# Another order table for a kernel of masked attention and a gated MLP

## The chip, the cores and the metric

The kernel runs on one core of a Trainium2 chip. The metric is the device time of one execution in microseconds (us). The kernel before takes 935.06 us, the median of three runs (934.54 to 935.51).

## The reference

The kernel computes masked attention, with two kinds of masks, and then a normalised, gated MLP over all 4608 tokens, all in f32:

```python
B, H, S, D = 8, 8, 576, 64                 # batch, heads, positions, head size
scores = q @ k.T / sqrt(D)
mask_local   = (rel >= 0) & (rel < 32)     # heads 0 to 3; rel = row - column
mask_strided = (rel >= 0) & (col % 32 == row % 32)   # heads 4 to 7
attn = softmax(where(mask, scores, -1e9))
x = (attn @ v), heads side by side         # 4608 tokens x 512
rms = sqrt(mean(x * x, axis=-1) + 1e-6)
xn = x / rms * rms_g
g = xn @ w_gate                            # 512 x 1536
silu = g / (1 + exp(-g))
out = (silu * (xn @ w_val)) @ w_out        # 1536 x 512
```

## The kernel before

**The work.** A core has five engines with a queue each: PE (matrix products), DVE and POOL (element by element), ACT (functions of one operand, copies) and SP (which here issues transfers). The attention is done in 32 iterations of one batch and two heads each. An iteration has the scores on PE (`scores`, L289), a softmax (`soft`: mask L309, maximum L312, exponentials on ACT L316, reciprocals of the sums L320 and L321, product L323, transpose L325) and the product with the values on PE (`values`, L301). What comes out is copied into three ring buffers `raw`, as chunks of 512 tokens. Nine chunks then go through the MLP. For each, the squares are added over the four column slices (`ssq`, L422), the row statistics are formed on PE (L431), followed by a root and four reciprocals (L484), and each slice is scaled (L488) and split into a high and a low part (xh and xl; for chunk 0 L508 and L515), since each f32 product is done as three products of parts.

**The MLP.** The first chunks use plain products. For each of twelve units of 128 columns there is a gate product and a value product (`gemm1`, L541), the gate's scaling for chunk 0 (L551), tanh on ACT (L554), the gate (L556), the product with the values (L592) and its split (L599 or L601, and L608), and then the output product (L617). For chunk 0, one more PE product spreads the row statistics over all rows (L472), and ACT copies it out (L475) for L551. While chunk 0 runs, the weights are still decoded: for each weight tile some bit operations on DVE (L1747 and L1752), the high part on ACT (L1757) and the low part by a subtraction (L1759), after which SP stores the tile to DRAM (L1763, the output weights wos at L1766). Later chunks go in pairs, which need seven products instead of eight, with sums and differences of weights made on the way: `transform_gv` (L668, L672) and `transform_o` (loads L800 and L806, sums L808), split at L756 and L762 and stored to DRAM (tg, L770). In these pairs the products stand at L1594, copies and sums of results at L1612 to L1649, and copies of weights at L1303, L1309 and L1368. The chunks at the end have similar lines from L901 to L1170.

**The order.** Every operation is put into a list, with the tiles it reads and writes, and with one or several engines that can do it (`op` in `Plan`; `also` names the others). For each step the table `ORDER` names which of the operations that are left comes next, and on which engine, and the kernel's instructions are issued in that order: each engine works through its own instructions in it. So the table sets three things, the place of each instruction in its engine's queue, the engine of those operations that have a choice (most of DVE's and POOL's element operations and many copies of ACT), and the order of the transfers on SP. It was encoded as text and is read in `order`:

```python
code = zlib.decompress(base64.b85decode(ORDER))
left, out = list(range(n)), []
for k in range(n):
    i = left.pop(code[k] + 256 * code[n + k])
    out.append(self.ops[i][0][ENGINES[code[2 * n + k]]][2])
```

Of the kernel before, what the change touches and what calls it, by code (L numbers as in the profile page):

```python
# [25 lines left out]
P = 128  # L26
# [37 lines left out]
    "Dh7t2KA{&wcm3oB8uM^0x=ye87J5bS|`CyD|X$AC;f9Px!C;_N%wgymbFdFP=s($K{uf<Q{r9eDImj+E^=CPx%{99fXg62L$W>V~;N1eB}D%wcOH^k3C^M9$HtXgB#Yh"
    "r5oScTDrRX#;J4Pau%*^E;yGi4mjtpHqTAD-j&UXP48mi!dT&)+xT|==84?!mUn%{+vtvUgTc$*@Md)6e6+GYG`AT&JaFm4z=cjcefG@s>8R1E)E}rkI6QD-{lp=Ec<5"
    "*?t{*Pf4j(@BFKe|!>;77}u^8@OsMMF2Dof49%4#*7Z^d)frMMB-N6O*u>IaRxv)#sY<Ne8A<Gu0mcgI&6W6Q1m<&}D~zEr5!_7rL#6=$l?m*eNke=$*c=9&0P{LbaK<"
    "M7h+w{ZC5QmN6%7f)@~tU`SI)OTa&nacP5@^{PeccKa{8pWuPFWrc?2BSg{MnMz?`JkLH6{GyATEOl%!qUkTN5bIPnPB;6!M-Ti$S<A<gZsm3GdL0i>-nKlaIn~k+J)9"
# [1833 lines left out]
```

## Time and profile before

| | |
|---|---|
| median of three runs | 935.06 us (934.54 to 935.51) |
| the profiled execution, its own time | 938.68 us |
| its span | 936.9 us |
| instructions | 21775 |
| mean granted clock of PE | 0.983 of full speed |

The profile is of one execution. Times in it are counted from the start of its span. An engine's busy time is the time in which it had an instruction under way. A timeline's row is an instruction, or a run of equal ones (x2): its start, its time, its engine, line, operation and tiles, and in brackets how long the engine had been idle before and what ended that. Where this text speaks of the 2.4 and the 1.2 GHz of PE, these are granted clocks of 1.0 and 0.5.

### The profile page before, as it was taken

To read this page: it belongs to the slowest core of one execution; us is meant where nothing else is said; L and a number is where in the kernel's file an instruction comes from. 1 tells how busy PE (TensorE), PEld (TensorE's weight loads), DVE (VectorE), ACT (ScalarE), POOL (GpSimd) and SP (SyncE) were. 2 spreads that over 40 slices of the span, in tenths; PEclk is the share of its full clock that TensorE was granted. 3 is DMA by queue.
4 is the path that set the end of the run, shared out by engine and by line. 5 is a ranking of instruction groups with operands and counts; after the bars stand their busy time and mean duration, and the time that the engine had idled before them with its cause. 6 is when DMAs were issued, how large, how long until landed. Compare 5 with 4: busy or idle time off the path is not lost.

```text
span 936.9 us, 21775 instructions
## 1 busy us (share of the span) xinstructions
PE 907.5 (97%) x8708; PEld 733.7 (78%) x8708; DVE 758.8 (81%) x1224; ACT 464.9 (50%) x1312; POOL 263.0 (28%) x220
## 2 busy tenths in 40 slices
PE   4999998999999999999999999999999999999998
PEld 3877876877788787888887878888888888888786
DVE  5999998879978999897668999536569994458893
ACT  6898774434335468354344675433445642232210
POOL 1322231224413344445016224200170241112320
PEclk7699999999999999999999999999999999999999
DMA  8797338695766888936884579765564796575643
GB/s 287 273 366 265 114 119 310 241 347 199 257 249 200 287 288 262 377 132 216 278 295 137 175 249 328 273 245 175 191 223 153 233 344 222 183 267 194 202 157 112
DMA packets 95092, 220.76 MB, mean 236 GB/s; under 512 B 9616, under 2 KB 28688, under 8 KB 94992
## 3 DMA queue, kind: packets, MB, share of 16 engines
q1 hardware_dynamic: 94560, 218.83, 67.4%
q8 instruction: 68, 1.11, 0.5%
q10 hardware_dynamic: 432, 0.56, 0.2%
q14 instruction: 32, 0.26, 0.1%
HBM read 172.17 MB, written 47.19 MB: 234 GB/s over the span
## 4 chain that ended last, share of the span: by engine, by line
PE 66%; DVE 10%; DMA 2%; issue 1%; ACT 1%; POOL 1%; SPq 0%; DVEq 0%; ACTq 0%; POOLq 0%
PE acc L1594 10%; PE acc L1393 7%; PE v L1594 6%; PE g L1594 6%; PE g L1393 5%; PE v L1393 5%; PE g L1005 3%; PE v L1005 3%; PE acc L1005 3%; PE acc L541 3%; PE v L541 2%; PE v L1170 2%; PE g L1170 2%; PE pair L289 2%; PE acc L1170 2%; PE g L541 2%
## 5 line engine op out<-in xcount | busy, mean ns | idle before, releaser
L541 PE MATMUL g<-xh,wg 128*128 128x512 f32 x184 | 60.9, 413 | 6.8 <-DVE e L556 6.8
L316 ACT ACTIVATE pT<-pT,mx 128x64 f32<-128x64 f32 x160 | 53.6, 339 | 23.1 <-DVE mx L312 23.1
L541 PE MATMUL v<-xh,wv 128*128 128x512 f32 x184 | 57.9, 396 | 0.3 <-DVE e L592 0.3
L316 ACT ACTIVATE pp<-pp,mx 128x64 f32<-128x64 f32 x160 | 53.6, 340 | 8.8 <-DVE mx L312 8.7
L541 PEld LDWEIGHTS g<-xh,wg 128*128 128x128 f32 x184 | 35.4, 198 | 16.3 <-DVE e L556 8.8
L289 PEld LDWEIGHTS pair<-xx,xx 64*32 64x32 f32 (+1 forms) x2432 | 28.0, 109 | 19.4 <-issue 12.0
L289 PE MATMUL pair<-xx,xx 64*32 64x64 f32 (+1 forms) x2432 | 34.2, 234 | 7.0 <-issue 3.1
L541 PEld LDWEIGHTS v<-xh,wv 128*128 128x128 f32 x184 | 33.8, 188 | 8.0 <-DVE e L592 0.9
L541 PE MATMUL g<-xl,wg 128*128 128x512 f32 x92 | 37.1, 403 | 0.0
L541 PE MATMUL v<-xl,wv 128*128 128x512 f32 x92 | 35.9, 390 | 0.0
L672 POOL TENSOR_TENSOR tt<-tt 128x256 f32<-128x256 f32 (+1 forms) x25 | 20.8, 840 | 48.6 <-DVE tt L672 28.4
L541 PE MATMUL acc<-xh,wg 128*128 128x512 f32 x104 | 33.7, 406 | 0.8 <-DVE hl L556 0.8
L541 PE MATMUL acc<-xh,wv 128*128 128x512 f32 x104 | 33.4, 402 | 0.0
L359 ACT COPY raw<-pair 128x128 f32<-128x128 f32 (+8 forms) x60 | 19.3, 370 | 26.5 <-PE pair L301 26.4
L617 PE MATMUL acc<-or,hh 128*128 128x512 f32 x96 | 30.2, 396 | 0.8 <-DVE e L556 0.8
L316 ACT ACTIVATION_READ_ACCUMULATOR pp<-pp,mx 128x1 f32 x160 | 30.7, 192 | 0.0
L316 ACT ACTIVATION_READ_ACCUMULATOR pT<-pT,mx 128x1 f32 x160 | 30.6, 191 | 0.0
L1594 PE MATMUL acc<-wg,wv 128*128 128x512 f32 x102 | 29.1, 394 | 0.0
L1594 PE MATMUL acc<-wv,wv 128*128 128x512 f32 x102 | 28.7, 389 | 0.0
L1612 ACT ACTIVATE or<-g 128x512 f32<-128x512 f32 x24 | 14.4, 599 | 21.9 <-PE g L1594 18.2
L301 PEld LDWEIGHTS pair<-pp,vt 32*64 32x64 f32 x784 | 18.1, 139 | 8.8 <-issue 6.2
L554 ACT ACTIVATE e<-g 128x512 f32<-128x512 f32 x23 | 13.8, 599 | 22.3 <-PE g L541 17.4
(860 smaller groups left out, 2936.1 us busy)
## 6 DMA issues: line engine op xcount, KB each, us to landing
wv<-wsv SPq DMA_DIRECT2D x36, 512.0 KB, 6.9
wg<-wsg SPq DMA_DIRECT2D x26, 512.0 KB, 7.5
or<-tg SPq DMA_DIRECT2D x22, 512.0 KB, 5.8
th<-tg SPq DMA_DIRECT2D x21, 512.0 KB, 6.5
tl<-tg SPq DMA_DIRECT2D x21, 512.0 KB, 6.2
xx<-in_qT_dram SPq DMA_DIRECT2D x32, 288.0 KB, 5.3
xx<-in_kT_dram SPq DMA_DIRECT2D x31, 288.0 KB, 6.1
wg<-wos SPq DMA_DIRECT2D x32, 256.0 KB, 4.8
```

The costliest lines, as they stand in the source:

```text
L289: nc.tensor.matmul(out=pair_[32 * y:32 * y + m, h, 64 * g:64 * g + 64], lhsT=q[r, PAD + a:PAD + a + m], rhs=k[r, a:a + 64], start=True, st ...
L301: nc.tensor.matmul(out=dst[z // 2][64 * h:64 * h + 64, z % 2, 320 + c:320 + f], lhsT=v[r, 6 * h + j], rhs=t[r, a:a + f - c], start=j == fi ...
L316: nc.scalar.activation(out=tv[:, g], in_=tv[:, g], func=AF.Exp, bias=m[:, g:g + 1], accum_out=z[:, g:g + 1])
L359: nc.scalar.copy(out=d, in_=s)
L541: nc.tensor.matmul(out=out, lhsT=wt[:, w, sl], rhs=xhl[x, kc], start=(n == 0 and i == 0), stop=(n == KC - 1 and i == 2))
L617: nc.tensor.matmul(out=acc[t], lhsT=x[h][:, sl], rhs=wt[:, w], start=(u == 0 and i == 0), stop=(u == NU - 1 and i == 2))
L672: elementwise(width, lambda e: both(e).tensor_tensor(out=dst(), in0=a(), in1=b(), op=ALU.subtract), [], keys)
L1005: nc.tensor.matmul(out=banks[bk], lhsT=w, rhs=X[a, k].tile(y), start=start and k == 0 and i == 0, stop=stop and k == 1 and i == 2, skip_gr ...
L1170: nc.tensor.matmul(out=banks[bks[j]], lhsT=tile(v, k, j), rhs=x.tile(y), start=start and k == 0 and i == 0, stop=stop and k == KT - 1 and ...
L1393: nc.tensor.matmul(out=banks[bks[j]], lhsT=w.tile(v, k, j), rhs=x.tile(k, y), start=start and n == 0 and i == 0, stop=stop and n == KT - 1 ...
L1594: nc.tensor.matmul(out=banks[bk], lhsT=w, rhs=xtile(a, k, y), start=start and k == 0 and i == 0, stop=stop and k == 1 and i == 2, skip_gro ...
L1612: op("ACT", act(CH, True), 0, lambda: nc.scalar.activation(out=temp(dst), in_=banks[bk], func=AF.Copy, scale=scale), reads=bank_keys(bk), ...
```

## The change

The table `ORDER` is replaced. The new text is 56 lines long where the old had 57, so that every line behind it has a number lower by one. The 3612 operations, the tiles and the engines that each can use are the same; 358 operations are on another engine, and in each queue places change. The diff, cut to the first lines of the table, whose text tells a reader nothing by itself:

```diff
 ENGINES = ("PE", "DVE", "ACT", "Pool", "SP")
 ORDER = (
-    "c-rk)*>fDnd7nP#zILuXXD{q777OCO2m%B_kRU*c6iMjdO@fqY5)7?_vTQ37C0nu%$C50`vJ#a;>ONvwNja`c;#BN%Ra}+#yre2m`3q8c$wQvf(>=4G-t&?wG<GqVp6;"
...
+    "c-rk)S(jYZbw2wHcb><ZtGcSXyLukf>XB|qprIupK}$jiB!L9N!ZaX^g)Bp2GiZUq3^L1xfN?OyU<L<59OohN%F5y)$wMBqR(?nFmX(*Bd(OSpt^5JM^u5(x_ug~PK70"
...
```

PE's queue near the start, before: in the program's names xh0 and xl0 are the two parts of the first slice of chunk 0, xh2 and xl2 those of the next; wg0 and wv0 the first unit's weights; L301 the value products of an iteration.

```order
L289 MATMUL pair_72<-xx4_84,xx3_83 32x64 x36
L541 MATMUL acc2_70<-xh0_548,wv0_355 128x512 x2
L541 MATMUL acc2_70<-xl0_597,wv0_355 128x512
L541 MATMUL g_67<-xh0_548,wg0_532 128x512 x2
L541 MATMUL g_67<-xl0_597,wg0_532 128x512
L301 MATMUL pair_72<-pT0_97,vt0_85 64x32 x2
...
L541 MATMUL acc2_70<-xh2_618,wv0_355 128x512 x2
L541 MATMUL acc2_70<-xl2_665,wv0_355 128x512
L406 MATMUL v_68<-few_65,ssq_101 128x4 x4
L406 MATMUL v_68<-few_65,srt_102 128x4 x4
L541 MATMUL g_67<-xh2_618,wg0_532 128x512 x2
L541 MATMUL g_67<-xl2_665,wg0_532 128x512
```

The same two places now:

```order
L288 MATMUL pair_72<-xx4_84,xx3_83 32x64 x36
L540 MATMUL g_67<-xh0_535,wg0_529 128x512 x2
L540 MATMUL g_67<-xl0_542,wg0_529 128x512
L300 MATMUL pair_72<-pT0_97,vt0_85 64x32 x2
...
L540 MATMUL acc2_70<-xh0_535,wv0_549 128x512 x2
L540 MATMUL acc2_70<-xl0_542,wv0_549 128x512
L405 MATMUL v_68<-few_65,ssq_101 128x4 x4
L405 MATMUL v_68<-few_65,srt_102 128x4 x4
L540 MATMUL acc3_71<-xh1_759,wg1_560 128x512 x2
L540 MATMUL acc3_71<-xl1_773,wg1_560 128x512
```

The group on the first value weights (acc2 from xh0 and wv0) has moved from ahead of these value products to behind the next ones. On DVE the L1759 that finishes wv0 has moved from row 15 of the queue to row 47. Behind the two statistics products (L406) PE now goes on with another slice (xh1).

DVE's queue where PE's longest wait ends, before: tt, th0 and tl0 belong to the weight sums, ssq and srt to the statistics of chunk 1, g and e to the gate of chunk 0.

```order
L762 TENSOR_TENSOR tl0_1849<-tt_105,th0_1826 128x512
L422 TENSOR_TENSOR ssq_101<-ssq_101,srt_102 128x512
L309 SCALAR_TENSOR_TENSOR pp0_95<-pair_72,cb_63 128x640
L312 TENSOR_REDUCE mx0_73<-pp0_95 128x10
L808 TENSOR_TENSOR tt_105<-tt_105,or4_1818 128x512
L484 RECIPROCAL srt_1949<-srt_1949 128x128 x3
L551 TENSOR_TENSOR g_67<-g_67,tl1_99 128x512
L672 TENSOR_TENSOR tt_105<-tt_105 128x256 x2
L556 SCALAR_TENSOR_TENSOR e_100<-e_100,g_67 128x512
L592 SCALAR_TENSOR_TENSOR e_100<-e_100,v_68 128x512
```

The same piece now:

```order
L421 TENSOR_TENSOR ssq_101<-ssq_101,srt_102 128x512
L761 TENSOR_TENSOR tl0_1861<-tt_105,th0_1857 128x512
L308 SCALAR_TENSOR_TENSOR pp0_95<-pair_72,cb_63 128x640
L311 TENSOR_REDUCE mx0_73<-pp0_95 128x10
L483 RECIPROCAL srt_1954<-srt_1954 128x128 x3
L550 TENSOR_TENSOR g_67<-g_67,tl1_99 128x512
L483 RECIPROCAL srt_1954<-srt_1954 128x128
L555 SCALAR_TENSOR_TENSOR e_100<-e_100,g_67 128x512
L591 SCALAR_TENSOR_TENSOR e_100<-e_100,v_68 128x512
```

The sum of squares comes ahead of the split, the L808 and the two L672 have left this piece, and the fourth reciprocal stands between L550 and L555.

SP's queue at the loads of the output weights wos2 and wos3, which the weight sums need, before:

```order
L1763 DMA wsg0_119<-wg0_532 128x1024
L800 DMA tt_105<-wos2_109 128x2x256
L770 DMA tg7_150<-th0_1826 128x1024
L800 DMA tt_105<-wos3_110 128x2x256
L1763 DMA wsv5_130<-wv5_1075 128x1024
```

And now:

```order
L272 DMA vt0_85<-in_vl_dram 128x768
L799 DMA tt_105<-wos2_109 128x2x256
L799 DMA tt_105<-wos3_110 128x2x256
L769 DMA tg7_150<-th0_1857 128x1024
L262 DMA xx0_80<-in_kT_dram 128x576
```

The second load has moved ahead of the store of tg7.

## Rows read from the trace of the kernel before

**Rows 1.** The page: span, and each engine's busy us, share, instructions.

```profile
span 936.9 us, 21775 instructions
...
PE 907.5 (97%) x8708; PEld 733.7 (78%) x8708; DVE 758.8 (81%) x1224; ACT 464.9 (50%) x1312; POOL 263.0 (28%) x220
```

**Rows 2.** Stretches: us, busy PE, PEld, DVE, ACT, POOL, PE clock, DMA, GB/s.

```profile
0.00:50.00 50.00, 36.52 (x800) 29.00 (x801) 37.71 (x79) 38.27 (x126) 11.82 (x24) 0.73 0.80 289
50.00:150.00 100.00, 93.32 (x1064) 72.49 (x1062) 95.45 (x149) 80.06 (x207) 25.72 (x20) 1.00 0.62 216
150.00:200.00 50.00, 47.99 (x427) 38.80 (x428) 41.48 (x70) 20.72 (x76) 13.59 (x14) 0.97 0.82 293
200.00:650.00 450.00, 447.08 (x4874) 361.78 (x4873) 376.88 (x602) 225.50 (x690) 145.42 (x112) 1.00 0.71 245
650.00:700.00 50.00, 50.00 (x296) 41.13 (x296) 30.50 (x49) 21.06 (x54) 19.32 (x15) 1.00 0.62 205
```

**Rows 3.** Timeline from 147 to 152 us: DVE, then ACT, then PE.

```profile
147.76 0.70 DVE L551 TENSOR_TENSOR g<-g,tl 128x512 f32<-128x512 f32 x1 [0.45 <-PE g L541]
149.66 0.88 DVE L672 TENSOR_TENSOR tt<-tt 128x256 f32<-128x256 f32 x2 [1.20 <-POOL tt L808]
150.46 0.68 DVE L556 SCALAR_TENSOR_TENSOR e<-e,g 128x512 f32<-128x512 f32 x1
...
151.78 0.94 DVE L484 RECIPROCAL srt<-srt 128x128 f32<-128x128 f32 x1
...
148.49 0.60 ACT L554 ACTIVATE e<-g 128x512 f32<-128x512 f32 x1 [0.85 <-DVE g L551]
...
151.20 1.20 PE L541 MATMUL g<-xh,wg 128*128 128x512 f32 x2 [3.48 <-DVE e L556]
```

**Rows 4.** Stretches around changes of PE's clock, columns as in rows 2.

```profile
31.80:38.60 6.80, 6.58 (x195) 5.91 (x186) 6.47 (x12) 5.89 (x16) 1.04 (x1) 1.00 0.61 190
38.60:45.40 6.80, 6.80 (x21) 5.64 (x21) 6.21 (x20) 6.05 (x11) 3.00 (x2) 0.50 1.02 405
...
151.20:154.60 3.40, 3.40 (x8) 2.72 (x9) 3.37 (x6) 1.14 (x2) 0.94 (x2) 0.51 0.97 360
```

**Rows 5.** Timeline of PE, and a row of DVE, from 28 to 48 us.

```profile
28.65 1.22 PE L541 MATMUL acc<-xh,wv 128*128 128x512 f32 x2
...
39.88 1.20 PE L541 MATMUL g<-xh,wg 128*128 128x512 f32 x2
...
45.98 1.05 PE L472 MATMUL acc<-pT,few 128*128 128x128 f32 x8
...
47.69 0.70 DVE L551 TENSOR_TENSOR acc<-acc,tl 128x512 f32<-128x512 f32 x1 [1.69 <-ACT tl L475]
```

**Rows 6.** Timeline of DVE at 190 and of PE at 198 us.

```profile
189.75 0.69 DVE L808 TENSOR_TENSOR tt<-tt,or 128x512 f32<-128x512 f32 x1 [4.14 <-DMA tt<-wos]
...
197.78 0.73 PE L541 MATMUL g<-xh,wg 128*128 128x512 f32 x2 [0.81 <-DVE e L556]
```

**Rows 7.** Timeline of PE: four single waits after 200 us.

```profile
253.85 0.73 PE L541 MATMUL acc<-xh,wg 128*128 128x512 f32 x2 [0.75 <-DVE hl L556]
...
498.92 0.72 PE L1594 MATMUL g<-xh,or 128*128 128x512 f32 x2 [0.88 <-ACT or L1612]
...
511.40 0.50 PE L1594 MATMUL v<-xh,th 128*128 128x512 f32 x1 [0.79 <-DVE tt L1644]
...
870.06 0.96 PE L1170 MATMUL acc<-wg,wv 128*128 128x512 f32 x3 [0.53 <-DVE hl L1035]
```

**Rows 8.** DVE and POOL at 54 us; groups of DVE, 50 to 150: busy us, mean ns.

```profile
54.28 1.83 DVE L1752 SCALAR_TENSOR_TENSOR th<-or 128x512 uint32<-128x512 uint32 x1
...
54.27 1.30 POOL L1759 TENSOR_TENSOR wg<-tt,wg 128x512 fp32r<-128x512 f32 x1 [2.75 <-ACT wg L1757]
...
L1752 DVE SCALAR_TENSOR_TENSOR th<-or 128x512 uint32<-128x512 uint32 x11 | 8.7, 787 | 0.3
...
L1752 DVE SCALAR_TENSOR_TENSOR tt<-wg 128x512 uint32<-128x512 uint32 x8 | 5.4, 678 | 0.1
```

More of the change, by code (lines that the diff above doesn't have):

```diff
@@ L64 @@
[L64 to L67, printed above, removed]
@@ new lines @@
+    "7~xA!fCS*ZKEY7yO1bd50bASL|U(_HPIA84nZ(X7bQnBlocH;p5za#>N8^ZGg6dq~j~$7bZDYo0NvMvXgz^BYH1)%VnclXP;wGHyG^Za+ZxIgGCTw`I~`-@g9|13E}=Y"
+    "k2>4Ta&UqjFoSz?5d29xK%Qj{%6}6OwCToG2>=0b!^|PN0#5L{7W!Yx4!NEVIlr~?Qh#PYqqsN`N}H)uKrp4dF{(j|G4nUKg8AQ$A3@%@KN&ZugCs*sQgcZAN;Z0{W2-"
+    "FKdZj;Y4xj5CcbKYO~3f-FXAshAN@S8_kL?eI{kP!(CEOgK6v~7_dj0ytEBQ#bK=8aP58h3CGCFD{fqZU=H7hoW$)t8I}2|Q&)*E+NUnIVb-mSBZr=U!%<XS>e){^pj{"
+    "j=7`0~r?IC(cvUU+YWc~@?>pL{bt^Hy;9r%wEnXZ+~F8&5xY;?)=055=!+RPVY$&NSWUPnUnRSg($(|Dg43@0siF-OsH)?T$Tj`<18CeTSa#H#d(S-21%;FQ@*MCn`_)"
@@ new lines @@
+    "k9(!>dTW={dmr@{9t$3OX!YUBg^Rlv8xI8KbH{@F?z{N#+=YwL-026VS?}!8`x3GloSulD7(MyO$xC}5E??Sncq%v)otwDyov5{RCK(+}*3S33XE%C@eedkFcVej8Y#u"
+    "*8a92EVtWs~TA6{Q?R%+|(hvM3P@YTJ+{PB8etrWy7K|H;f?ru*0Zf>%fHl{vVYBthxTpvkhI<=vhca!RPw>tK-@lh7`SgE==xG-2PEhg!FnCuFlOQ(OB#_uN4=+*f9B"
+    "gyyPIGbEa?tAsV>#u}yT&ulse|)lfDSoJ;m!oT?(!X6TRn(}IcuBk&hv}n(!FQ4{jl+vk7=@K{l_(89n<|ILV?7AQ%YmQzNhdkvA3Sx)Kj7cJKlYCW{?Q<*4jl?g-QW&"
+    "C92w}X4Xk!LD=RCVc&Y6-hXQ|(@3&VxueDh5=1bmOEtpM$>FHo9IO<Kbz4ZleG>mp>b$8J9b<eh)UTjay&bs5%u083r?Xgp1?r3Wy=_T{SiCY_tJFRNn+k4P!ta-f)r4"
@@ new lines @@
+    "?^2wUf^BylwNvVcn@YRi|P{rJ>s30hf<B14$Y?jg}WWb+_i)ZrR>nvh5^s?Nujqyq53S?rqMlk)@iqd)nUZI%w9mtZCAl3`SppG2=$fd$DR5gO?nmV;k3FYu1Xbz%V_}"
+    "Ok6iAn@g6laM{;)hjVUQpBeD=rp-#ua%!{KV%<(ijn@8lYanR*0}X$s*)s0b^>H@ECe_30dZNXXd*U^HRc$k+McE>)(_QTvtv2c8M1_u1I!Z@WIvlC1Azh)%{!+NsY_{"
+    "m~{L(yKXwZQ=g-T_NSfeG<`(H9NPNv7m;#jKfCPO2X3=cDMHzA$o?@1dDe?3rd9BV2AxP@!AdL#Yl-|M(msp478{xzMNnMx<aVLTMDE_iJKm}uH#H(nfjeys5y<D-8*2"
+    "BTp0p!XqM>kgGW4Hzi30ES@jjYn9m1j;w9@`ZN#)k_2a$cO5m(bHanuhrb>$dO6}zVFAL?}P2S&fr_6E_6C@&YvHEnKNeV9>bY{x&>B6D_?8DIyCgUo^0x2^k}pUq2lj"
@@ new lines @@
+    "S=O3KyMBdpAzco>AswKGUB-C|mJB9)801obGz+Pwh=T&FLST#-=izjXv_(<gH7>-OtV2%g-4Vdr{a#rzXxH5<}tfV!i5o@-FS;=4<YR5h`=Ht?l(s4{!T&=t9n!ATtc5"
+    "FqpNDHwM8;hRdHf+x^P>Tzgz|O|=kwdy2xJny?rb~^(V9^rYx1W$Ow)Q+?t(@1Emg@_i$L?K-g53u5Vr3GA)+Pe-DD<$lj8x{~1=^rLwrkTAPm+^niA)%zH>#5%?Q1;f"
+    "tMnV>MD)|J`kPuv!6Yf@34TwDrXmgBsk%3@qL4|Zj5AMh3A3SX4wwY%a~QPgR2x=f)eis0bd69&WrZ0k)4psgYN{wcOIgSqL_Ol&ebZDlKe80}fTuXTJ`qYx<<A1D>Mo"
+    "mOL@ilUREwUbn;O016AwSa7ZPNu4?SQY&>9HctGrKu{^d#fixVjDfxhDs6yUcV{8oth3>R7|C@yHMe7&V!gV^}Kq3}|s{vCbXrq*`@O1&?5<)b=nX{P;a?fx3oKc+3FA"
@@ new lines @@
+    "$239uHsNTK^D1b`i@BqV(Ucv(U+R@xuy|^C`4EEYdScHDNhmhB+`h>9EZKmEJ7TN;Raan0y6*%0>^)d2_gVGfCf*3`na;sA&jo-bcJY3Q~`7zHvqvI1%RP3WPfNA@|zD"
+    "Zyw5F0<QK@oZ`X8$G_<C?wrWtcjPynC1q^@~Ll_avXDvOA78&ACFjnytnjC$~xQZwq-ml(~UbgWjVk@ZbKa9x5%Ir<O`t5vGt&mA|a%>VEUsrG#A{bP?ZbZ=D0Q(IZRx"
+    "RYumVDGi#zd^g1A*Qg9@QIz`dGu*7&2Nz!)U(Q?cRa3#=>;7<X0ER{jy(5t<>7vwG35nEp&UAduG>bo7&hZ%~aLasF$8jy;JI3L)Xhy{cwHFs;kLDY0V7Rh7wcj%yI7@"
+    "Hk_$s4Aq!pjv>EmT{mJ1Hk#8ai%nWHloT^Ga+yZZ>ycp#xd_@inD$-kCISO&1!`t$u9m^T98=2!yKQB*X_AFWglh(#s!WaG$-Bx^p3+U<=_*S6wyIF}CT(ago>ouT3nf"
@@ new lines @@
+    "*J)E^UXhG@@{gN}-@8L|3m$i3~g<~_=g&11_r;;2Vk!<d*{di@)YtTsza3PZF43UG#?2(WG2U<ayc>Z+|<>gyJt#yb;51x75BkQxU?nHS@PhaOY_PiJri7+|Xgl&7l3R"
+    "HgvyQtj*z0r%cE5R(AbK>dVUYJtr_Hz=cuV^ScXE@*Em*k-R`YD}w?>MwQ}5KJ&UYjSLX${=RMphQs#3wYK7MwXSWw2=zPL?%a<#s`U|k#(YK2!Ek)MCn8)9P^AdGeA!"
+    "fg<F^{)42)MB8ci7bci8@G6*8zVv&hCWI3vxT`-HZXHBH3XiU`<1?jA7YwSs@VIHg>sCpOg*#C%i+r@or<^w6SR~KW0*H)%`b2`&CWLnfv5Ft=n#q6cQPSRlvx8_?op!"
+    "%#gt@m)Xn+#XlY5CGHxd>4g*BVWX8v1E?&PPzPH&QqW$Klu!h49qiscYd$jueKMSJb5xo!dA~muyBC2Ta&)+zAW&>jdG-o}b{c^$`pQNTS|O+9YhTk!Ekc(;8|vflfi~"
@@ L104 @@
+    "Bx3fjuKqA*NmoKTnuK7*~|D>x1JftklAr%Wk3kGX_gW-;21QxUTq=m@s*f@VpHF)G@!9N{umGS5(2JS-XqK3$fYBE9l8TQCyX%a&8<H=L6A<jaHr4hTWFJVG+nvU^!Xa"
+    "lcyR6@ug)%~tzO#IH5*|JtxypNnfrQ=}-`NK$>#TIPI*^A=3LyY#Cj^bsLpL1m9yyu)O@plrX9q@pdn=f5ZA-JaYQ<s^dS75zUY3fd?"
 )
```

55 lines of the change are left out of this document (16 added, 39 removed).

## The prediction

> **What bounds the kernel now.** I read the page first, then the busy time by stretch, then PE's waits, then single rows. TensorE (PE) is busy 907.5 us of a span of 936.9 [rows 1], and its instructions are the same 8708 after the change, so a new order can only take out PE's idle time, 29.4 us, or PE time at the half clock, or add to either. The table of stretches says where the idle time lies [rows 2]: 50.00 − 36.52 = 13.5 us in the first 50 us, 6.7 us from 50 to 150, 2.0 us from 150 to 200, 2.9 us in the whole of 200 to 650, nothing from 650 to 700. The reader should see that three quarters of it lies before 200 us.
>
> From 50 to 150 VectorE (DVE) is busy 95.45 of 100 us, PE 93.32 [rows 2]: there DVE sets the pace and PE waits for it. After 200 the sides change: DVE has 450.00 − 376.88 = 73 us of slack to 650, PE 2.9. So an operation that moves costs or pays before 150, and after 200 only where it stands ahead of something that PE waits for.
>
> **The change, part by part.** No operation goes or comes. 358 of 3612 change engine: DVE gets 6 operations more, ScalarE (ACT) 5 more, GpSimd (POOL) 11 fewer. At 0.68 us on DVE and 1.30 on POOL for 512 columns [rows 8] that is some 4 us more on DVE and 14 fewer on POOL, out of 758.8 and 263.0 [rows 1]. Over the whole span engine time is not what it is about.
>
> *The stop at 151.* PE's longest wait, 3.48 us, ends with the gate product L556 on DVE [rows 3]. The chain behind it is L551 on DVE (from 147.76), tanh on ACT (148.49 to 149.09), L556. L556 could start about 149.4, but in DVE's queue two L672 stand ahead of it, which wait 1.20 us for a POOL addition, so it starts at 150.46: 1.06 us lost. The new order has neither L672 there; a reciprocal (0.94 us) stands in the tanh's time instead, which is as long with its hand-overs. And L551, which waits for PE, comes sooner, since the sum of squares L422 now precedes L762, worth one instruction of 0.7, and one L808 leaves DVE's queue ahead of the reciprocals. 1.06 + 0.7: **−1.8**. Bounds: 0.7 (L556's part alone, less an overhang of the reciprocal) and 3.5 (all of the wait).
>
> Behind that stop the granted clock is 0.51 for 3.40 us [rows 4], the 1.2 GHz level of the two, after PE had been idle 3.48 us. If the stop shrinks to 1.7 us the fall may not come: 3.4 us of work at half clock is 1.7 us lost. The waits of 0.75 to 0.88 us later in this trace [rows 7] bring no slice of the page to the half clock; 1.7 lies between 0.9 and 3.5, nearer the first, but it follows a stretch in which PE waits often. I take 0 and keep −1.7 as an end.
>
> *Startup.* PE's group on the first value weights, at 28.65 us [rows 5], now stands behind the fourth value products (about 35.4), since DVE finishes that weight's low part 32 rows later. The first group on the second input slice moves up ahead of L472 in its place. Five groups ran from 39.88 to 45.98, 1.22 us each at half clock. One group more at full clock is 0.68, less what PE gains by the one that has gone at 28.65: I put L472 0.3 us later, and DVE waits for its result (1.69 us at 47.69, by way of ACT) [rows 5]. From there to 150 DVE paces, so it is passed on: **+0.3**. Ends: −1.0 (that wait of 1.69 partly closed) and +6.4 (the slower rival below).
>
> *The output weights at 190.* DVE's L808 waits 4.14 us for the second half of a weight tile (wos), whose load SyncE (SP) issued behind a 512 KB store [rows 6]; SP now issues both loads ahead of that store. PE's wait of 0.81 us at 197.78 [rows 6] is on an L556 at the end of DVE's row of work from there: **−0.8**. Ends: 0 and −0.8.
>
> *Single waits later* [rows 7]. At 253.85 PE waits 0.75 us for an L556 behind a softmax product (L323) on DVE that moves to POOL: −0.7. At 498.92 ACT's L1612 stood behind a weight copy (L1303) that now stands elsewhere, and at 511.40 DVE's L1644 stood behind an addition (L1368) whose place changes: of 0.88 + 0.79 I take two thirds, −1.1, since other work takes the places. At 870.06 an L1035 stood behind L901 and L908, and DVE has 6 us less to do in this stretch: −0.5. Ends for the four together: 0 and −2.9.
>
> *650 to 700.* Twelve operations go from POOL to DVE: 12 × 0.69 = 8.3 us. DVE has 19.5 us idle there and PE none [rows 2]: 0. Without that cover, each of the twelve ahead of one that PE waits for, it would cost the 8.3 us.
>
> *New waits.* 358 changed engines and a local reshuffle cannot only close waits. The old order lets 2.9 us through in the 450 us from 200 [rows 2]. I add something under half of that, **+1.3**, ends 0 and +4.
>
> Sum: −1.8 + 0.3 − 0.8 − 0.7 − 1.1 − 0.5 + 1.3 = −3.3 us. The profiled execution took 938.68 us, 1.8 more than its span and 3.6 above the median of 935.06; I take the difference to the median: 935.06 − 3.3 = 931.8.
>
> **What speaks against it.** At 54.28 an L1752 on DVE takes 1.83 us, where a group of the same form has a mean of 678 ns; POOL's L1759 ran from 54.27 for 1.30 us [rows 8], and DVE ended 0.54 us after it. Another group of the form has a mean of 787 ns over 50 to 150 [rows 8]; four such groups, 39 instructions, exceed 678 by 0.11 us each, 4.3 us in all, beside 25.72 us of POOL's work [rows 2]: 0.17 us for each us. The order puts two or three operations, about 3.5 us, more on POOL there, where DVE paces: 0.6 us by that ratio, 3.5 if every one is hit. The new waits and the range take this in.
>
> The Trainium skill, "SBUF — State Buffer", section "Who interferes with whom", states that DVE and GpSimd share a port under an exclusive lock, and that the second to issue fully blocks. The 1.83 us agrees with that; by the rule alone the 3.5 us would come back, and the sum would be about +0.2.
>
> **The rivals.** *No change:* POOL's operations from 50 to 150 block DVE for 1.9 us (about midway from 0.6 to 3.5), and displaced waits reach 2.3 instead of 1.3: −3.3 + 1.9 + 1.0 = −0.4, 934.7. For it: DVE's 95% there. Against: the stop at 151 comes from a queue's order, not from DVE's load. Chance 0.26.
>
> *Faster still:* the clock holds at 151 (−1.7) and no new waits come (−1.3): −3.3 − 3.0 = −6.3, 928.8. For it: the stop is halved. Against: two things must both go well. Chance 0.16.
>
> *Slower, at the start:* at 28.65 two instructions of PE take 1.22 us against 1.20 at 151 at the clock of 0.51 [rows 3, 5], so it ran at half clock; from 31.80 to 38.60 the clock was full, 6.58 us of it busy, and then it fell to half for 6.8 us [rows 4]. The group at 28.65, dense work just before the clock rose, has gone from there. If the clock stays at half through the next 6.58 us, they take up to 6.4 us more. From 50 to 150 DVE's idle time away from the stop, 4.55 − 1.65 = 2.9 us [rows 2, 3], could return part of it; I take none, since its queue stands behind the same PE results. The sum is −3.3 + 6.4 = +3.1, 938.2. It decides once the startup lies more than 3.3 + 1.9 = 5.2 us behind. Against it: the gate group and the value products still stand there. Chance 0.16.
>
> That the table does nothing is excluded: the queues differ from the first rows on.
>
> **How the numbers follow.** My forecast, 931.8, has 0.42, its own range 930.0 to 933.1. From 928.0 to 937.0 lies all of it, all of the no-change case and about half of each outer one. About 0.2%, 1.9 us, is what a measurement of this kernel can tell from no change: faster means under 933.2, slower over 936.9. Faster is 0.42 + 0.16 = 0.58, same 0.26, slower 0.16.
>
> **What would show it.** In the changed profile (line numbers one lower): PE's wait on L555 near 150 should be under 2 us; the rows at 197.78 and of [rows 7] should have lost their waits; PE should be busy over 446 of the 450 us from 200 to 650; L471 should start by 46.5. The forecast is wrong if the clock from 32 to 38 shows 0.5, if DVE instructions of 0.69 us show 1.3 and more between 50 and 150 more often than before, or if PE's waits after 200 add up to over 5 us.

## The result, and the profile after

The changed kernel takes 927.51 us (median of 6 runs, 924.45 to 931.18), the kernel before, beside it, 935.28 (934.42 to 937.08). The ratio is 0.9915 with a 95% interval of 0.9888 to 0.9942, so it is faster by 7.8 us; 3.3 us were forecast, and 927.51 lies below the range of 928.0 to 937.0. A second set of six runs gave 928.73 (ratio 0.9910, 0.9882 to 0.9937). One correction to what stands above: the table has 44 lines before and 43 after, not 57 and 56; the shift of the line numbers by one is right.

The profiled execution of the changed kernel took 924.45 us, 3.1 below its median; that of before 938.68, 3.4 above the 935.28. So the two traces differ by 14.2 us where the kernels differ by 8. What a trace shows of single places is told as such below, and what they are worth from the runs. A second trace of the changed kernel (after_again, 925.84 us) is called in where the two differ.

The page of the changed kernel has these lines for [rows 1]:

```profile
span 922.5 us, 21759 instructions
...
PE 901.5 (98%) x8708; PEld 732.7 (79%) x8708; DVE 741.0 (80%) x1226; ACT 467.3 (51%) x1321; POOL 248.3 (27%) x209
```

The stretches of [rows 2] from 50 us on, in the same columns, and the waits of PE behind 50 us (total us, times, longest):

```profile
50.00:150.00 100.00, 97.61 (x1081) 77.14 (x1080) 95.96 (x159) 79.62 (x205) 31.26 (x25) 0.98 0.78 275
150.00:200.00 50.00, 50.00 (x602) 40.61 (x601) 42.78 (x73) 25.54 (x102) 13.17 (x12) 1.00 0.73 255
200.00:650.00 450.00, 449.94 (x4737) 366.12 (x4736) 364.59 (x607) 225.41 (x691) 133.41 (x107) 1.00 0.71 243
650.00:700.00 50.00, 50.00 (x372) 41.08 (x371) 41.34 (x68) 21.16 (x54) 6.42 (x5) 1.00 0.57 183
```

```profile
PE g L540 <- DVE e L555: 2.2, 1, 2.2
```

From 50 to 150 PE is busy 97.61 instead of 93.32 us, while DVE's share hardly changes (95.96 against 95.45) and POOL has 31.26 us of work instead of 25.72. From 200 to 650 PE lacks 0.06 us where it lacked 2.9. Behind the startup one wait is left that the profile names, 2.2 us on L555 (the old L556); the trace of after_again has two more, 1.04 us at 82.46 and 0.58 us at 215.41. In 650 to 700 DVE has 11 us more to do, and PE has no idle time: that cover held.

The wait that is left, by engine (DVE, ACT, PE), against [rows 3]:

```profile
141.99 0.70 DVE L550 TENSOR_TENSOR g<-g,tl 128x512 f32<-128x512 f32 x1 [0.84 <-PE g L540]
142.59 0.94 DVE L483 RECIPROCAL srt<-srt 128x128 f32<-128x128 f32 x1
143.45 0.63 DVE L555 SCALAR_TENSOR_TENSOR e<-e,g 128x512 f32<-128x512 f32 x1
...
142.72 0.60 ACT L553 ACTIVATE e<-g 128x512 f32<-128x512 f32 x1 [1.17 <-DVE g L550]
...
144.14 0.73 PE L540 MATMUL g<-xh,wg 128*128 128x512 f32 x2 [2.19 <-DVE e L555]
```

L555 now starts 0.13 us after the tanh has ended, behind the reciprocal. PE waits 2.19 us instead of 3.48, and that is the chain of three instructions with its hand-overs. Most of the other traces have 2.14 to 2.25 us here.

To see where the two traces part, I take the start of PE's n-th instruction (PE has the same 8708 in both) and subtract before from after: −0.3 us at 50 us of the old trace, −5.8 at 147, −7.0 at 160, −8.2 at 210, −9.6 at 300, −10.4 at 490, −12.7 at 560 and −14.3 from 880 on. This difference is called the drift below.

The page lets the 14.4 us of span be split: PE's idle time went from 29.4 to 21.0 us, and its busy time from 907.5 to 901.5, at the same 8708 products and with 33 and 32 us of half clock in the two records. Some 4 of these 6.0 us lie behind 50 us. Much of that goes with the waits, for a wait costs more than its idle time. The old trace at the wait of 0.88 us:

```profile
496.53 0.84 PE L1594 MATMUL acc<-wg,wv 128*128 128x512 f32 x3
497.21 0.84 PE L1594 MATMUL acc<-wv,wv 128*128 128x512 f32 x3
498.92 0.72 PE L1594 MATMUL g<-xh,or 128*128 128x512 f32 x2 [0.88 <-ACT or L1612]
499.49 0.40 PE L1594 MATMUL g<-xl,or 128*128 128x512 f32 x1
499.72 0.62 PE L1594 MATMUL g<-xh,or 128*128 128x512 f32 x2
500.18 0.39 PE L1594 MATMUL g<-xl,or 128*128 128x512 f32 x1
```

Three products in a row take 0.68 us from start to start here (497.21 less 496.53), but 0.84 is shown for them (the profile models the ends of products), so 0.16 us of a wait that follows is booked as busy; and the first pair behind the wait takes 0.57 us to the next start, where the second takes 0.46. So this wait delays PE by about 0.88 + 0.16 + 0.11 = 1.15 us, and the drift moves by 1.17 there. For the wait of 0.79 at 511.40 it moves by 1.07, for that of 0.53 at 870.06 by 0.82. Behind 50 us the old trace has 15 waits of 0.15 us or more and the new one has 1, and 14 times 0.27 us would be 3.8 of the 4 us; that is an estimate. The 1.8 us of the startup are open.

### The profile page after: what moved, and what is told of

It reads as the page before. It is cut to its first block, busy times and chain, and to the rows that moved or that the text cites. A ratio compares the mean times of both kernels' runs of the same rounds, so it can differ in the third digit from the quotient of the medians.

```text
span 922.5 us, 21759 instructions
## 1 busy us (share of the span) xinstructions
PE 901.5 (98%) x8708; PEld 732.7 (79%) x8708; DVE 741.0 (80%) x1226; ACT 467.3 (51%) x1321; POOL 248.3 (27%) x209
## 4 chain that ended last, share of the span: by engine, by line
PE 94%; DVE 3%; DMA 1%; issue 1%; ACT 1%; SPq 0%; DVEq 0%
PE acc L1593 11%; PE acc L1392 8%; PE acc L540 7%; PE v L1593 7%; PE g L1593 7%; PE g L540 7%; PE v L540 7%; PE v L1392 5%; PE g L1392 5%; PE v L1004 4%; PE g L1004 4%; PE acc L1004 4%; PE acc L616 4%; PE pair L288 3%; PE pair L300 3%; PE v L1169 2%
## 5 line engine op out<-in xcount | busy, mean ns | idle before, releaser
L540 PEld LDWEIGHTS g<-xh,wg 128*128 128x128 f32 x184 | 34.5, 192 | 10.2 <-DVE e L555 2.9
L671 POOL TENSOR_TENSOR tt<-tt 128x256 f32<-128x256 f32 (+1 forms) x27 | 23.6, 879 | 68.9 <-DVE tt L671 61.0
L540 PE MATMUL v<-xl,wv 128*128 128x512 f32 x92 | 35.9, 391 | 0.0
L1611 ACT ACTIVATE or<-g 128x512 f32<-128x512 f32 x24 | 14.4, 598 | 22.8 <-PE g L1593 22.7
```

Source lines behind the costliest of these rows:

```text
L540: nc.tensor.matmul(out=out, lhsT=wt[:, w, sl], rhs=xhl[x, kc], start=(n == 0 and i == 0), stop=(n == KC - 1 and i == 2))
L671: elementwise(width, lambda e: both(e).tensor_tensor(out=dst(), in0=a(), in1=b(), op=ALU.subtract), [], keys)
L1611: op("ACT", act(CH, True), 0, lambda: nc.scalar.activation(out=temp(dst), in_=banks[bk], func=AF.Copy, scale=scale), reads=bank_keys(bk), ...
```

## The experiments

The kernels differ from one of the two by the table alone. Where a table was put together from both, the first steps are one kernel's, and the operations that are left then follow in the other's order.

**Halves.** 

```diff
h_new_then_old: ORDER
- the old table's steps
+ the new table's first 682 steps, then what is left in the old order
h_old_then_new: ORDER
- the old table's steps
+ the old table's first 682 steps, then what is left in the new order
```

> The new table's first 682 steps (to about 157 us of the old trace, just behind the stop at 151), then the rest in the old table's order and on the old engines. Places theory (the gain comes wherever an instruction that PE needs stood behind others in its queue, and half of it lies before 157 us, where the two profiles drift apart by 7.2 of 14.3 us): about half of the gain, 930.5 to 932.5 against 935.3, and PE's waits of 0.88 and 0.79 near 490 to 505 us come back. Rival, early part alone (after 157 us the old order had only 5.5 us of PE idle time, some of it modelled): nearly all of the gain, under 929.5.

> The mirror: the old table's first 682 steps, with the stop at 151, then the new table's order and engines. Places theory: the other half, 930.5 to 932.5, with the 3.5 us wait on L556 still there and hardly a PE wait behind it. Rival, early part alone: no change, 934 to 936.

The first took 934.73 us (ratio 0.9984, 0.9967 to 1.0001), the second 943.96 (1.0079, 1.0063 to 1.0095). Both expectations failed by their totals, and for reasons of their own. In the trace of the first, the drift is −6.7 at 155 us and between −6.6 and −7.1 from there to 850: the early half does its part, and the late waits come back (0.88 and 0.79 near 500 us), as the places theory said; but its runs spread from 930.97 to 937.67, with the profiled one near the lower end. In the second a stop arises at the seam, where a softmax comes late. Its waits of PE, with line numbers that are 13 higher in this file, begin with it:

```profile
PE pair L314 <- DVE pp L338: 9.0, 1, 9.0
```

Behind it PE is at half clock for 10.2 us. A table put together has a seam, and what the seam costs must be looked up before its total is read. Behind the seam PE is busy 449.00 of the 450 us from 200 to 650, so the new order closes the late waits without the new early part.

**Places or engines.**

```diff
o_new_places_old_engines:  order of the new table, engine of each operation from the old
o_old_places_new_engines:  order of the old table, engine of each operation from the new
```

> The new table's order of all 3612 operations, each on the engine that the old table gave it. Places theory: most of the gain stays, 927.5 to 931.5. Engines theory (the 358 switches, which take some 14 us off POOL and end blocked DVE instructions, are what pays): little is left, 934 or more. Since each order was made with its own engines, single waits will open in either case; a middling result says that the two belong together.

> The old table's order, each operation on the engine that the new table gives it. Places theory: no gain, 935 to 942, with the wait at 151 still 3 us or more. Engines theory: most of the gain, 927 to 931.

970.67 us (1.0372, 1.0346 to 1.0397) and 995.36 (1.0620, 1.0600 to 1.0641). Either half of the change alone is far slower than no change: in 200 to 650 PE is busy only 433.23 and 421.27 us. Places and engines belong together in this table, the two theories could not be told apart in this way, and the later experiments change single places.

**The startup.**

```diff
s_old54_then_new:     old steps 1 to 221, then new
s_new54_then_old:     new steps 1 to 221, then old
s_old_warm_then_new:  old steps 1 to 26, then new
s_old36_then_new:     old steps 1 to 139, then new
s_group_back: DVE's and PE's queues in the new table
+L1758 TENSOR_TENSOR wv<-tt,wv          (first value weights, now ahead of a transpose at 30 us)
 L324 STREAM_TRANSPOSE pT<-pT
-L1758 TENSOR_TENSOR wv<-tt,wv          (at 37 us)
+L540 MATMUL acc<-xh,wv x2, L540 MATMUL acc<-xl,wv    (now ahead of the first gate group)
 L540 MATMUL g<-xh,wg x2
```

> The old table's first 221 steps (to about 54 us), then the new table. In the two profiles the kernels stand 0.3 us apart at that point and the other 14 us come behind it, but the new kernel's runs spread from 924.5 to 931.2 and those that show more half clock are longer. Startup-clock theory (the new startup leaves PE at half clock for longer in part of the executions, which costs the median some 3 us): 921.5 to 924.5, with a spread of 4 us or less. Rival (the spread comes from behind the startup): 926 to 929, with a spread as wide as the new kernel's.

> The mirror: the new table's first 221 steps, then the old table. Startup-clock theory: slower than before by 1 to 4 us, 936 to 940, with a spread of 5 us or more, the longer runs at the lower mean clock. Rival: 934 to 937, like before.

> The old table's first 26 steps (the memsets, the first loads and PE's two warm-up products, which then begin 1.1 us later), and the new table from there. If the earlier warm-up is what lengthens the half clock: 922 to 925 with a small spread. If it is the later part of the startup (the value weights' group that moved from 28.65 to 37.85): 926 to 930 and a wide spread, as with the whole new startup.

> The changed kernel again, unchanged, on the same chip as the three above: 925 to 930 by median, runs from 924 to 932. Startup-clock theory: in a run of 929 us or more PE's clock is at half for 40 us or so of the first 60, against 27 in the profile of 924.45 us; rival: the longer runs have further half-clock stretches or waits behind 60 us.

> The old table's first 139 steps (to about 36 us, with the value weights' group at 28.65 in its old place), then the new table, which skips the seam at 60 to 70 us that cost the run with 221 old steps some 3 us. Startup-clock theory (the half clock of 41 us belongs to the group's new place): recorded half clock of 28 to 32 us in the runs, spread of 3 us or less, median 924.5 to 927. Rival (it belongs to what follows 36 us): half clock up to 41 us again, 927 to 931.

> The new table with one group moved: DVE's L1758 of the first value weights stands ahead of a transpose at about 30 us, and PE's group on them ahead of the first gate group, as in the old table. Startup-clock theory: as in the run before this one, no run with 41 us at half clock, 924 to 927. Rival: the group's place does not matter, half clock up to 41 us, 927 to 930 and a spread of 5 us or more.

| kernel | median us (runs) | ratio, interval |
|---|---|---|
| s_old54_then_new | 929.84 (929.11 to 931.27) | 0.9927, 0.9903 to 0.9952 |
| s_new54_then_old | 937.09 (932.83 to 940.03) | 1.0009, 0.9987 to 1.0031 |
| s_old_warm_then_new | 930.20 (927.38 to 931.70) | 0.9925, 0.9897 to 0.9954 |
| after_again | 928.73 (925.84 to 930.93) | 0.9910, 0.9882 to 0.9937 |
| s_old36_then_new | 927.62 (926.48 to 928.05) | 0.9892, 0.9866 to 0.9919 |
| s_group_back | 927.80 (926.16 to 928.98) | 0.9895, 0.9870 to 0.9920 |

The new startup alone (s_new54_then_old) costs or gains nothing that can be measured. But it makes the runs uneven. Five of its twelve have a mean clock of 0.976 to 0.978, which at 936 us is 41 to 45 us at half clock, and took 938.7 to 940.0; the others with a whole clock record have 28 to 36 us and took 932.8 to 937.0. The new kernel shows the same: 31 us in runs of 924 to 926 us, 37 in two of 927.5, 39 to 41 in runs of 928 to 930. (A clock near 1.00 beside a long time does not contradict it: in the profile of s_old36_then_new, with 0.996, the record only begins at 32 us.) With the value weights' group back at its place (s_group_back), and with the old first 36 us, no run has more than 35 us, and the spread falls from 6.7 us (5.1 in the second set) to 2.8 and 1.6. With the first 26 old steps alone it does not: five of six runs have 37 to 41 us. Its profile (930.37 us) shows where: half clock from 9.6 to 36.9, from 40.3 to 47.1 and from 149.5 to 152.9 us, where that of the change has 8.5 to 35.9 and 145.1 to 148.5. Over all runs with a whole record, 37 us or more at half clock occur in 20 of 35 with the group at its new place (the change in both sets, h_new_then_old, s_new54_then_old and s_old_warm_then_new), in none of 18 where the new table follows the old start or has the group moved back, and in 7 of 74 of the old kernel, though not all of these were run side by side. So the group's place makes the longer half clock more frequent, and is not its only cause. The startup-clock theory was right in that and wrong in the price: the ratios of the two kernels, 0.9892 and 0.9895, are only a little below the new kernel's 0.9915 and 0.9910, with intervals that overlap widely. The 929.84 of the first row contains new waits at its seam (1.46 us at 62.92 and 0.95 at 69.08; the drift goes from −1.8 at 60 to +1.4 us at 70).

**What POOL does to DVE.**

```diff
l_no_pool, POOL's and DVE's queues in the old table
-19 operations of POOL from 50 to 141 us
+the same on DVE, at the same steps
```

> The old table, with the 19 operations that POOL has between 50 and 141 us on DVE, at the same places. It measures what POOL's work does to DVE. By their free lengths the 19 are some 13 us more for DVE, which paces there. Lock theory (the 6.0 us by which DVE's instructions from 50 to 141 us exceed their usual length come from POOL's instructions beside them): the excess falls under 1.5 us and the kernel is 6 to 9 us slower, 942 to 946. Rival (the excess comes from transfers or from ACT): it stays at 4 us or more, and the kernel is 12 us slower or more.

940.93 us (1.0041, 1.0017 to 1.0065), less than the 942 to 946 expected. Here is a group of DVE between 55 and 150 us (busy us, mean ns), of the old kernel and then of this one:

```profile
L1747 DVE SCALAR_TENSOR_TENSOR or<-or 128x512 uint32<-128x512 uint32 x10 | 8.0, 797 | 0.0
```

```profile
L1747 DVE SCALAR_TENSOR_TENSOR or<-or 128x512 uint32<-128x512 uint32 x10 | 6.8, 684 | 0.0
```

Without POOL's work no group is long. For the sums I take PE's 822nd to 1860th instruction (55 to 147 us in the old trace) and call excess what DVE's instructions take over the usual duration of their form (which duration is taken as usual shifts all these sums together, by up to 1 us). The old kernel has 5.0 us of it, this one 0.6, though DVE works off some 11.5 us more by usual durations. So the excess is POOL's doing. And the 17 to 19 operations that POOL takes in this stretch save PE only 3.0 us (the stretch is 95.0 against 92.0 us): 0.16 to 0.18 us each, where each is 0.6 us of DVE's time.

**The neighbours of POOL's instructions.** In the old trace one sees which instructions of DVE are long: at 89 us (DVE, then POOL)

```profile
88.65 0.82 DVE L309 SCALAR_TENSOR_TENSOR pp<-pair,cb 128x640 f32<-128x640 f32 x1
89.38 1.73 DVE L1747 SCALAR_TENSOR_TENSOR wg<-wg 128x512 uint32<-128x512 uint32 x1
91.03 0.81 DVE L312 TENSOR_REDUCE mx<-pp 128x10 f32<-128x640 f32 x1
...
89.26 1.30 POOL L1759 TENSOR_TENSOR or<-th,or 128x512 fp32r<-128x512 f32 x1
```

L309 overlaps POOL and has its usual length; L1747, which starts 0.12 us after POOL, is done only after it. In the new trace three of POOL's instructions in a row stand beside others:

```profile
86.73 0.82 DVE L308 SCALAR_TENSOR_TENSOR pp<-pair,cb 128x640 f32<-128x640 f32 x1
87.58 0.82 DVE L311 TENSOR_REDUCE mx<-pp 128x10 f32<-128x640 f32 x1
88.32 0.68 DVE L555 SCALAR_TENSOR_TENSOR e<-e,g 128x512 f32<-128x512 f32 x1
89.10 0.69 DVE L591 SCALAR_TENSOR_TENSOR e<-e,v 128x512 f32<-128x512 f32 x1
...
85.57 1.80 POOL L1758 TENSOR_TENSOR wg<-tt,wg 128x512 fp32r<-128x512 f32 x1 [6.88 <-ACT wg L1756]
87.33 1.30 POOL L1758 TENSOR_TENSOR wv<-tt,wv 128x512 fp32r<-128x512 f32 x1
88.59 1.30 POOL L1758 TENSOR_TENSOR or<-th,or 128x512 fp32r<-128x512 f32 x1
```

All of DVE's keep their length: L308, L555 and L591 have one operand in PSUM, L311 has only one. Over the stretch the new trace has 19 POOL instructions instead of 17, and an excess of 2.7 us instead of 5.0; in the trace of after_again it is 1.1 us higher than that.

One operand is not always enough. In the old trace L320, which has one operand of ten columns and usually takes 0.17 us, lasted until POOL was done:

```profile
196.00 0.94 DVE L320 TENSOR_SCALAR mx<-su 128x10 f32<-128x10 f32 x1
...
195.62 1.28 POOL L762 TENSOR_TENSOR tl<-tt,th 128x512 fp32r<-128x512 f32 x1 [2.27 <-DMA xx<-in_kT_dram]
```

A CAST of L756 took 0.96 us at 192.67 beside POOL's L672 instead of its usual 0.42. The Trainium skill, "SBUF — State Buffer", section "Who interferes with whom", states that a DVE instruction with two SBUF inputs contends with a GpSimd instruction that reads SBUF, and that one with at most one SBUF input does not, outside the 2-port performance modes, which copy, cast and tensor_scalar can enter. The trace agrees: 1.73 us with two SBUF inputs, 0.82 and 0.68 us with one, and 0.96 and 0.94 us for the CAST and the TENSOR_SCALAR.

Then single exchanges in the old table:

```diff
 l_one_pair, DVE at 54 us           l_four, DVE at 54, 80, 89 and 115 us
 L1747 or<-or                       -L1752 th<-or    +L1752 th<-or behind L592
+L556 e<-e,acc                      -L1747 or<-or    +L1747 or<-or behind L592
 L1752 th<-or                       -L1747 wg<-wg    +L1747 wg<-wg behind L312, L556
-L556 e<-e,acc                      -L1752 tt<-wv    +L1752 tt<-wv behind L551, L309, L1747, L312
 L592 e<-e,v                        l_three: the first three of these
                                    ACT's copy L1757 of tt goes along (56 us; in l_four 117 us too)
```

> The old table with a single exchange on DVE at 54 us: L556, which reads a product in PSUM and for which PE waits 0.81 us at 56.76, now stands ahead of L1752, which has two operands in SBUF and took 1.83 us beside POOL's L1759. Places theory: PE's wait there goes, and the drift against the old kernel's trace at 60 us is -1 us or so, kept to 140 us as far as L1752 is now done in 0.7 us (934 to 935.5 by median). Rival (DVE has no slack there, each us that it works comes back at the next wait): the drift is back to within 0.4 us of zero by 100 us.

> The old table with four exchanges on DVE between 54 and 120 us: an L1747 or L1752, all of whose operands lie in SBUF and which took 1.7 to 1.8 us beside a POOL instruction, changes places with the two to four instructions behind it that read a product in PSUM or have one operand (L556, L592, L312, L551, L309). If the new table's gain from 54 to 147 us is that its POOL work stands beside such instructions (DVE's excess there 5.0 us in the old trace, 2.7 in the new): the excess falls to 1.5 to 3 us and the drift at 147 us is -2 to -4, 933 to 935 by median. Rival (only the whole order does it; the blocked time goes to the next instruction, as in the single exchange): excess 4 us or more, drift at 147 us within 1 us of zero, 936 to 937.5.

> The old table with the first three of the four exchanges (at 54, 80 and 89 us), without the one at 115, behind which three new collisions and a wait of 2.98 us arose. Up to 110 us the run with four had brought the excess from 3.2 to 1.0 us and the PE stretch from 54.9 to 52.1. Block theory: the 2.8 us stay to 147 us, and the median is 933.5 to 935 against 937. Rival (what is won before 110 us is lost at the next collisions anyway): drift at 147 us within 1 us of that at 55, 936 to 937.5.

The single exchange gave 936.90 us (1.0004, 0.9982 to 1.0025). Its DVE at 54 us:

```profile
54.16 0.68 DVE L556 SCALAR_TENSOR_TENSOR e<-e,acc 128x512 f32<-128x512 f32 x1
54.76 1.34 DVE L1752 SCALAR_TENSOR_TENSOR th<-or 128x512 uint32<-128x512 uint32 x1
```

L556 is no longer late, but L1752 still starts while POOL runs (54.26 to 55.55) and waits for it: 0.5 us are saved, and the drift is back at −0.2 by 70 us. Its rival was right. A second neighbour is needed to fill POOL's 1.3 us, and l_four has at least two behind each exchange.

l_four: 936.93 us (1.0007, 0.9993 to 1.0020). To 110 us it did what was expected (excess 1.0 instead of 3.2 us, no wait at 56, 82 and 92 us, the drift from −0.9 at 55 to −3.7). Then its fourth exchange undid it. Two of the three places, on DVE, POOL and PE:

```profile
118.32 1.78 DVE L1747 SCALAR_TENSOR_TENSOR wg<-wg 128x512 uint32<-128x512 uint32 x1
...
121.62 1.91 DVE L323 TENSOR_TENSOR pT<-pT,mx 128x640 f32<-128x640 f32 x1
...
117.88 1.67 POOL L668 TENSOR_TENSOR tt<-wv 128x512 f32<-128x512 f32 x1 [3.95 <-DVE wv L1759]
121.58 1.27 POOL L608 TENSOR_TENSOR hl<-e,hh 128x512 fp32r<-128x512 f32 x1 [2.03 <-ACT hh L599]
...
124.51 0.77 PE L301 MATMUL pair<-pT,vt 32*64 32x32 f32 x21 [2.98 <-issue]
```

Three other instructions with two operands in SBUF now met POOL, and the values product that needs the L323 came 2.98 us late, with a fall of the clock behind it.

l_three, without the fourth: the drift goes from +0.2 at 55 us to −2.5 at 110 and stays, −2.3 at 147 and −3.0 at the end. The stretch of PE is 89.5 us instead of 92.0. In the runs it is 935.68 us against 937.22 (0.9983, 0.9965 to 1.0001), which is less than expected and not clear of no change. So that the neighbours are worth time is shown in the trace, and only made likely by the runs.

**The predicted terms.**

```diff
p_terms, old table
 DVE, 150 us:  +L556, L592 ahead of the two L672
 SP, 183 us:   second L800 (wos3) two steps sooner, but still behind L770 (tg7)
 DVE, 253 us:  +L556 hl ahead of L325
 ACT, 498 us:  +L1612 ahead of L1303
 DVE, 511 us:  +L1644 ahead of L1368
 DVE, 868 us:  +L1035 ahead of L908
c_both_parts: these and the exchanges of l_three
```

> The old table with only the moves that the prediction's terms behind the startup rest on: the two L672 behind L556 and L592 at 150 us; the second wos3 load ahead of the tg7 store; L556 ahead of the transpose at 253; L1612 ahead of L1303 at 498; L1644 ahead of L1368 at 511; L1035 ahead of L908 at 868. By the terms (1.06 where that wait occurs, 0.8, 0.75, 0.88, 0.79, 0.53) the trace should gain 3.5 to 4.8 us and the median 932 to 934 against 937, the gains adding up behind each other. Rival (what is repaired in one place is lost at the next wait, as at 54 us): the drift returns within 50 us of each place, 935.5 to 937.5.

> The old table with these three exchanges and with all the moves of p_terms: nine places in all. If the two parts are separate and are what the new table's gain consists of: 2.8 + 4.1 = 6.9, 929.5 to 931.5 against 937, where the new table stands at 928.5. Rival (they overlap, since both let DVE reach 147 us sooner): 932 to 934.

One of the moves did not take place. In p_terms and c_both_parts the second load of L800 still follows the store, as in the old kernel:

```profile
178.87 0.53 SPq L800 DMA_DIRECT2D tt<-wos  x1
179.50 0.55 SPq L770 DMA_DIRECT2D tg<-th  x1
180.50 0.53 SPq L800 DMA_DIRECT2D tt<-wos  x1
```

DVE's L808 still waits 4.01 us for it (4.14 before), and PE 0.69 us at 195.51 (0.81 before). So the term of the output weights was not tried by itself, and five moves were.

p_terms: 932.91 us against 937.05 (0.9961, 0.9945 to 0.9978), −4.1. The gains add up in the drift, which is −0.8 at 147 us, from the startup, −2.2 at 155, −3.2 at 260, −4.6 at 520, −4.9 at 880: after 150 us, where DVE has slack, most of what a move gives is kept. Of the waits that the moves were meant to close, 0.36 us is left at 495.40 and 0.30 at 866.84, and one of 0.50 us at 397.98 is new.

c_both_parts: 931.78 us against 937.22 (0.9951, 0.9932 to 0.9971), −5.4, a little above the range of the sum, with hardly an overlap in the trace (−2.5 us up to 147 and −3.7 behind). So eight places of the old table give two thirds of what the new one gives.

**Two more places in the new table.**

```diff
b_both, new table: s_group_back, and DVE at 77 us
 L1758 TENSOR_TENSOR wg<-tt,wg
+L555 SCALAR_TENSOR_TENSOR e<-e,g
+L591 SCALAR_TENSOR_TENSOR e<-e,v
 L1751 SCALAR_TENSOR_TENSOR tt<-wg
-L555 SCALAR_TENSOR_TENSOR e<-e,g
-L591 SCALAR_TENSOR_TENSOR e<-e,v
```

> The new table with the value weights' group back at its old place in the startup and, at 77 us, L555 and L591 ahead of an L1751 that took 1.67 us beside POOL. Places theory: the wait of 1.0 us near 82 us goes, 926 to 927.5 by median with a spread under 4 us, the fastest of all. Rival: back within 30 us, 927.5 to 929.

925.23 us (four runs, 923.98 to 927.02) against 937.05: 0.9875, 0.9858 to 0.9892, and less than the 926 expected at the least. That is 0.35% under the ratio of after_again, with intervals that overlap a little (0.9882 to 0.9892); the two were not run side by side. Nor do the runs tell the exchange on DVE from the group's place, which gave 0.9895 (0.9870 to 0.9920) by itself in s_group_back. The L1751 that took 1.67 us in the new trace, and what it is now:

```profile
77.57 1.67 DVE L1751 SCALAR_TENSOR_TENSOR tt<-wg 128x512 uint32<-128x512 uint32 x1
```

```profile
78.87 0.69 DVE L555 SCALAR_TENSOR_TENSOR e<-e,g 128x512 f32<-128x512 f32 x1 [0.26 <-ACT e L553]
79.66 0.69 DVE L591 SCALAR_TENSOR_TENSOR e<-e,v 128x512 f32<-128x512 f32 x1
80.27 0.69 DVE L1751 SCALAR_TENSOR_TENSOR tt<-wg 128x512 uint32<-128x512 uint32 x1
...
78.42 1.34 POOL L1758 TENSOR_TENSOR wv<-tt,wv 128x512 fp32r<-128x512 f32 x1 [8.97 <-ACT wv L1756]
```

## Why the prediction was wrong

The sign was right, and so were the places that the sum named; the size was not: 3.3 us forecast, 7.8 and 8.1 measured. The step that failed is that the sum gave nothing to the stretch from 55 to 147 us. By the steps, with the drift of the two profiled executions for each:

- *What speaks against it*: **this is the step that failed.** I had noted 6.7 us of PE's idle time from 50 to 150, but read DVE's 95% there as an amount of work that paces PE, gave the stretch only the stop at its end, and charged POOL's 3.5 us more of work (it became 5.5) by a mean of 0.17 us per us, up to all of it (the four groups of DVE that this mean rests on exceed 678 ns by 4.6 us in all, not by 4.3). The stretch from 55 to 147 us became 5.4 us shorter (92.0 to 86.6; 87.5 in after_again), and PE's waits in it, 0.81, 0.93, 1.19 and 0.70 us, two of 0.26 and one of 0.2, are gone (after_again keeps one of 1.04). Of DVE's account there, the excess fell by 2.3 us, its work by 1.5 and its idle time by 0.7; for the other 1.0 us its instructions follow each other more closely. POOL's work is not charged by its amount but by what stands beside it: 0.6 us of excess without POOL, 5.0 in the old order and 2.7 in the new with more of POOL's work. The waits at 56.76, 82 and 92 us I had seen as a sign of DVE's load and not as places; l_three moves three instructions there and gets 2.5 us of the 5.4 in its trace. From the section of the Trainium skill quoted above ("SBUF — State Buffer", "Who interferes with whom") I had taken the lock alone, and left out which instructions don't contend.
- *What bounds the kernel*: that an order can only change idle time and half-clock time was wrong as well. PE's busy time fell by 6.0 us, and some 4 of them go, by the estimate above, with waits that cost PE about 0.27 us each beyond the idle time shown.
- *Single waits later*, −0.7, −1.1 and −0.5: −1.1, −2.3 and −1.2. All four waits are gone in the profile of the change, so the third that I held back for other work in those places was held back for nothing, and each wait was worth more than its idle time.
- *The stop at 151*, −1.8: the wait went from 3.48 to 2.19 us, −1.3; the one on L422 (0.70) is gone too, and counts in the stretch above. That the L672 cost the 1.06 us I put on them isn't shown: in l_one_pair, l_three and s_new54_then_old, where the old order runs up to there after another start or early part, PE's wait is 2.17 to 2.22 us with the L672 in place, while h_old_then_new has 3.37. And "under 2 us" was wrong: the chain alone takes 2.19. That the clock may fall there or not was rightly left open: it fell behind 2.19 us in the profile of the change and not in that of after_again.
- *Startup*, +0.3: −0.3 in the trace (+1.3 in that of after_again), and 1.0009 (0.9987 to 1.0031) for the new startup alone. The clock was at half from 8.5 to 35.9 us without a break, where the old trace has 11.3 to 31.8 and 38.6 to 45.4: 27.3 us in either. So the sign that I had named, half clock between 32 and 38 us, came up to 35.9, without the loss of the slower rival.
- *Output weights*, −0.8: −1.2 in the trace, but that the order of the loads did it isn't shown. No run tried it by itself, and in l_one_pair, with the loads in the old order, the wait at 198 us is missing too (0.19 us at 217.65 stands in its place).
- *650 to 700*, 0: right, PE is busy 50.00 of 50.
- *New waits*, +1.3: this term failed too. From 200 to 650 PE has 0.06 us of idle time in the trace of the change and 0.64 in that of after_again, and none from 650 to 900. A share of the old order's waits is no estimate of the new one's.

p_terms shows five of these moves by themselves: −4.1 us by the runs (the interval is −2.1 to −5.2), against −3.4 in my sum for them (−1.1 for the L672, −0.7 − 1.1 − 0.5).

Of the rivals, "no change" rested on charging POOL's work by its amount, and fell with that. "Faster still" was nearest by its number, 928.8, and half right: new waits hardly came, but the clock held at the stop in the trace of after_again and not in that of the change, and its sum too had nothing for 55 to 147. So its number was luck. The slower one named something true, the group at 28.65 and the half clock, and had its price too high: it shows in part of the executions, as some 3 us (939 against 936 for s_new54_then_old), and not in the medians. What stays open is why a fixed order ends up with 31 or with 41 us at half clock, and some 2.5 us of the 8 that the eight places do not bring; the DVE work that the new table puts off from the stretch is a candidate that wasn't tried.

## What to carry to other kernels

Before an operation goes to POOL, look at what DVE does during its 1.3 us. In these traces it cost DVE nothing beside an instruction that reads PSUM or beside a TENSOR_REDUCE, and about 1 us beside one with two operands in SBUF (1.73 instead of 0.68), more than the 0.7 that it saves; a CAST or a TENSOR_SCALAR can be held up as well. A place in a queue that was repaired kept its gain behind 150 us, where DVE has slack, and lost it within 20 us at 54, where DVE paces; there several had to be repaired together, and a new collision undid them. A short wait of PE is worth about 0.27 us more than the idle time that a row shows. And when two profiles are compared, first place each execution among its kernel's runs: here the pair of traces showed 14 us where the kernels differ by 8.
